# Zero matmuls ahead of the first scores, and new figures in the planner that orders the kernel

## The chip, the cores and the metric

The kernel runs on one core of a Trainium2 chip. The metric is the device time of one execution in microseconds, taken over several runs; 0.2% of it is about 1.7 us. A profile of one execution, taken separately, gives the rows below. PE is TensorE, DVE is VectorE, ACT is ScalarE, POOL is GpSimd and SP is SyncE, which here issues the DMAs.

## The reference

Three steps follow one another, all in float32:

```python
# q, k, v: 4 x 8 heads x 576 x 64; a window of 64 positions
scores = q @ k.T / 8, with -1e9 outside 0 <= i - j < 64
attn = softmax(scores)                        # max taken off, sum + 1e-9
x = (attn @ v), heads side by side            # 2304 x 512
h = x @ w_in;  x = (h * clip(h + 3, 0, 6) / 6) @ w_out     # 512 -> 2048 -> 512
h = x @ w2_in; out = max(0.01 * h, h) @ w2_out             # 512 -> 2048 -> 512
```

The weights arrive as float64 and are rounded on the chip.

## The kernel before, in words

Every float32 product is made of three matmuls on two halves of each operand (`...h` and `...l`). The attention is cut into 20 items (`items`), each one or two groups of 64 query positions of one batch. For an item, `scores` multiplies keys by queries into one or two PSUM banks. For the first nine items (`EARLY`) a mask matmul (L494, `ident_r` times `mask_r`) writes the mask into the bank first, and the scores (L507) add to it. `softmax` then takes the maximum (DVE L466, L467), the exponential (ACT L455), the sum (DVE L476), its reciprocal (DVE L462, L463), and normalises on POOL (L343). `st_P` transposes (L532) and `st_V` multiplies by the values (L564). 

The first layer follows block by block of tokens. Six chunks of 128 of the 2048 inner columns are done plainly (`st_h` L617, `st_y` L663), with the attention of later blocks between them. Their weights are loaded (`st`), rounded by DVE and ACT (`rounded`, L370 to L389) and parted into halves (`halves`, L332 and L342). The remaining chunks and the whole second layer are done in pairs by a scheme with seven instead of eight products (`paired`, L943, L1037, L1086, L1211); halves made once are kept in DRAM and loaded again.

Nothing of this is issued in the order in which it is written. Each step is put into a list (`Order.op`) with the engines that can do it and a cost for each, what it reads and writes, a delay after its end, and `later`, a list of steps that must have started before it. `Order.forward` then plays the list: again and again it takes the engine that can start something first, and on it the ready step with the earliest due time. `Order.backward` makes new due times from the outcome, and six such rounds are made. The best one is emitted, sorted by planned start, and that is the program order of every engine, each of which takes its instructions strictly in turn. The semaphores come from elsewhere: a framework follows the emitted instructions and makes each wait for earlier accesses to the same bytes of a tile. The plan itself knows only the reads and writes that a step names.

The planner's figures: an instruction of n columns costs 0.19 + 0.00083 n on ACT, 0.15 + 0.00104 n on DVE (half the slope for copies and scalar operations), 0.2 + 0.0024 n on POOL. A step starts 0.15 us after a step on another engine that it depends on, and 0.12 after one on its own engine for DVE and POOL. A load is 0.62 us on SP, then its bytes at 0.36 MB per us on one DMA engine, then a delay of 2.0.

Tiles come from rings. A ring can have homes: places inside other tiles that are free early on. The key tiles (`kt`) have two buffers of their own and two homes, in the token tile `xb` that later holds the first layer's output:

```python
late = sum(SIZES[:NB - 2])      # 1536
"kt": heads([(("home",), None, lambda i=i: xb(i, late, NK3)) for i in range(2)])   # NK3 = 768
```

`xb(c, o, n)` (with `XT` = 768) is columns c * 768 + (o mod 768) and on of tile number o // 768; there are `NPAIR` = 3 such tiles. The first identity and mask are made in tile 0 (L1326 to L1338). At the start SP issues loads of keys and queries for items 0 and 1, for item 2, of keys for items 3 and 4 (into the homes), then values and the first weights. Queries have two buffers.

Of the kernel before, what the change touches and what calls it, by code (L numbers as in the profile page):

```python
# [17 lines left out]
class Order:  # L18
# [5 lines left out]

    BIAS = 10.0
    LAG = 0.15

    class Buf:
        def __init__(self, pool, shape, dtype, tag, bufs):
# [32 lines left out]
    def op(self, ways, reads=(), writes=(), delay=0.0, chain=False, later=()):  # L62


        i = len(self.ops)
        deps, behind = set(), set(later)

        def whole(x):
            return x[0] if isinstance(x, tuple) and isinstance(x[0], self.Buf) else x

        def touch(b):
            if not b.ops:
                if b.prev is not None and b.prev[0] is not None:
                    behind.add(b.prev[0].ops[0])
                if b.prev is not None and b.prev[1] is not None:
                    deps.update(b.prev[1].ops)
            elif b.ops[0] != i:
                behind.add(b.ops[0])
            if not b.ops or b.ops[-1] != i:
                b.ops.append(i)  # L80

        for x in (*reads, *writes):
            b = whole(x)
            if isinstance(b, self.Buf):
                touch(b)
                if b.parent is not None:
                    touch(b.parent)
                if b.home is not None:
                    self.hist.setdefault(b.home, ([], []))[1].append(i)
        for x in reads:  # L90
            w, r = self.hist.setdefault(x, ([], []))
            deps.update(w)
            r.append(i)
        for x in writes:
            w, r = self.hist.setdefault(x, ([], []))
            deps.update(w + r)
            w.append(i)
        if chain:
            if self.last is not None:
                behind.add(self.last)  # L100
            self.last = i
        deps.discard(i)
        behind.discard(i)
        self.ops.append((ways, sorted(deps), sorted(behind - deps), delay))

    def lag(self, a, b):
        return (0.12 if a in ("DVE", "POOL") else 0.0) if a == b else self.LAG

    def forward(self, due):


        ops, after = self.ops, self.after
        n = len(ops)
        left = [len(deps) + len(behind) for _, deps, behind, _ in ops]
        ready, free, done, start, used = {}, {}, [0.0] * n, [0.0] * n, [0] * n

        def push(i):
            ways, deps, behind, _ = ops[i]
            for k, w in enumerate(ways):
                t = 0.0  # L120
                for d in deps:
                    t = max(t, done[d] + self.lag(ops[d][0][used[d]][0], w[0]))
                for d in behind:
                    t = max(t, start[d])
                ready.setdefault(w[0], {})[i] = (t, k)

        for i in range(n):
            if not left[i]:
                push(i)
        for _ in range(n):  # L130
            while True:
                e, t = min(
                    ((e, max(free.get(e, 0.0), min(x[0] for x in q.values()))) for e, q in ready.items() if q),
                    key=lambda x: x[1],
                )
                q = ready[e]
                i = min((j for j, x in q.items() if x[0] <= t), key=lambda j: (q[j][0] if e == "DMA" else due[j], j))
                r, k = ready[e][i]
                ways, _, _, delay = ops[i]
                best = min(  # L140
                    range(len(ways)), key=lambda m: max(free.get(ways[m][0], 0.0), r, t) + ways[m][1] + self.BIAS * m
                )
                if best == k:
                    break
                del ready[e][i]
            for w in ways:
                ready.get(w[0], {}).pop(i, None)
            start[i], used[i] = max(t, r), k
            free[e] = start[i] + ways[k][1]
            done[i] = free[e] + delay  # L150
            for s in after[i] + self.then[i]:
                left[s] -= 1
                if not left[s]:
                    push(s)
        return start, used, max(done)

    def backward(self, start, used, end):
# [8 lines left out]
        def push(i):  # L166
            t = end - ops[i][3]
            for s in after[i]:
                t = min(t, late[s] - self.lag(eng[i], eng[s]) - ops[i][3])
            for s in then[i]:  # L170
                t = min(t, late[s] + cost[i])
            ready.setdefault(eng[i], {})[i] = t
# [4 lines left out]
        for _ in range(n):  # L177
            e, t = max(
                ((e, min(free.get(e, end), max(q.values()))) for e, q in ready.items() if q), key=lambda x: x[1]
            )  # L180
            i = max((j for j, x in ready[e].items() if x >= t), key=lambda j: (start[j] + cost[j], j))
            del ready[e][i]
            late[i] = free[e] = t - cost[i]
            for d in ops[i][1] + ops[i][2]:
                left[d] -= 1
                if not left[d]:
                    push(d)
# [36 lines left out]
def swa_relu6_leaky_kernel(ctx: ExitStack, tc: tile.TileContext, q, k, v, w_in, w_out, w2_in, w2_out, out):  # L224
# [14 lines left out]
    nc = tc.nc  # L239
# [79 lines left out]
    def act(n, fn):  # L319
        return ("ACT", 0.19 + n * 0.00083, fn)  # L320

    def dve(n, fn, fast=False):
        return ("DVE", 0.15 + n * (0.00052 if fast else 0.00104), fn)

    def pool(n, fn):
        return ("POOL", 0.2 + n * 0.0024, fn)

    def pe(t, fn):
        return ("PE", t, fn)
# [9 lines left out]
        )  # L339

    def tensor_tensor(n, dst, a, b, alu, last=True):
        d = dve(n, lambda: nc.vector.tensor_tensor(out=dst(), in0=a(), in1=b(), op=alu))  # L342
        p = pool(n, lambda: nc.gpsimd.tensor_tensor(out=dst(), in0=a(), in1=b(), op=alu))  # L343
        return (d, p) if last else (p, d)

# [2 lines left out]

    def load(bytes_, dst, src, writes, reads=(), later=()):
        op([("SP", 0.62, lambda: nc.sync.dma_start(out=dst(), in_=src))], reads, writes, later=later)  # L350
        op([("DMA", bytes_ / 3.6e5, lambda: None)], (), writes, delay=2.0)

    def store(bytes_, dst, src, reads, writes):
        op([("SP", 0.62, lambda: nc.sync.dma_start(out=dst, in_=src()))], reads, writes)
        op([("DMA", bytes_ / 3.6e5, lambda: None)], reads, writes, delay=2.0)


    EXP_LO = float.fromhex("0x1.2p-15")
# [3 lines left out]
    def rounded(src, later=()):  # L362
# [14 lines left out]
        def af():  # L377
# [7 lines left out]
        op([ts(a, a, 3, 0x3FFFFFFF, ALU.logical_shift_left, ALU.bitwise_and)], [a], [a])  # L385
        op([dve(DM, lambda: nc.vector.scalar_tensor_tensor(  # L386
            out=a(), in0=high(), scalar=0xC0000000, in1=a(), op0=ALU.bitwise_and, op1=ALU.bitwise_or
        ))], [a, st], [a])
        op([act(DM, lambda: nc.scalar.activation(  # L389
            out=r(), in_=st()[:, :, 0], func=AF.Copy, scale=2.0 ** -29  # L390
        ))], [st], [r])
# [41 lines left out]
    def softmax(L, pp, early, apart):  # L433
# [24 lines left out]
                    **({} if apart else {"accum_out": sm()[:, c:c + 1]}),  # L458
                )

        def recips():
            nc.vector.tensor_scalar(out=rc(), in0=sm(), scalar1=1e-9, scalar2=None, op0=ALU.add)  # L462
            nc.vector.reciprocal(out=rc(), in_=rc())  # L463

        def greatest():
            nc.vector.tensor_reduce(out=nb(), in_=p3(), axis=AX.X, op=ALU.max)  # L466
            nc.vector.tensor_scalar(out=nb(), in0=nb(), scalar1=-SCALE, scalar2=None, op0=ALU.mult)  # L467

        if early:
            op([("DVE", 0.31 + NP * L * 0.00104, greatest)], [pp], [nb])  # L470
        else:
            op([("DVE", NP * (0.23 + L * 0.00104), low)], [pp], [s, nb])
        src = [pp, nb] if early else [s, nb]
        if apart:
            op([("ACT", NP * (0.2 + L * 0.00083), exps)], src, [s])
            op([dve(NP * L, lambda: nc.vector.tensor_reduce(out=sm(), in_=sv(), axis=AX.X, op=ALU.add))], [s], [sm])  # L476
        else:
            op([("ACT", NP * (0.3 + L * 0.00083), exps)], src, [s, sm])
        op([("DVE", 0.35, recips)], [sm], [rc])
        op(tensor_tensor(NP * L, sv, sv, lambda: rc().unsqueeze(2).to_broadcast([P, NP, L]), ALU.mult, False),  # L480
           [s, rc], [s])
        return s, sv
# [1 line left out]
    def scores(n, pps):  # L484
# [8 lines left out]
        for pp in pps if early else ():  # L493
# [1 line left out]
                pp()[:, 0:NP * L].rearrange("p (c l) -> p c l", c=NP), ident_r,  # L495
                mask_r[:, P - L:P].unsqueeze(1).to_broadcast([P, NP, L]), start=True, stop=True,
                skip_group_check=True,
            ))], writes=[pp])

        def fn():  # L500
            for c in range(NP):
# [10 lines left out]

        return 0.25 + NP * 0.222 * L / P, fn, [x, y], pps

    def st_S(n, pps):
        cost, fn, reads, writes = scores(n, pps)
        op([pe(cost, fn)], reads, writes)
        softmaxes(n, pps)

    def softmaxes(n, pps):  # L520
# [82 lines left out]
    def st_h(idx):  # L603
# [28 lines left out]
        def gg():  # L632
# [11 lines left out]
        op(copy(n, gg, rr, True, 1.0 / 6.0), [r], [gh])  # L644
        op([dve(n, lambda: nc.vector.scalar_tensor_tensor(
            out=gl()[:, 0:n], in0=rr(), scalar=1.0 / 6.0, in1=gg().bitcast(F32), op0=ALU.mult, op1=ALU.subtract
        ))], [r, gh], [gl])
        gs[idx] = (gh, gl)

    def st_y(idx):  # L650
# [161 lines left out]
    def paired():  # L812
# [340 lines left out]
        def outputs2(p, n, pairs):  # L1153
# [104 lines left out]
                todo.append(go)  # L1258
            return todo

        kk = 0
        turn_ = 0
        todo, plan = [], FILL[0]
# [56 lines left out]


    zero = const.tile([P, 1], F32, name="zero")
    nc.vector.memset(zero, 0.0)
    nc.scalar.activation(out=zero, in_=zero, func=AF.Exp)
    ident_f, mask_f = xb(0, 0, P), xb(0, P, P)
# [28 lines left out]
    for b in range(1, NB):  # L1354
        of[b] = [n for n in of[b] if n not in of[b - 1]]
    ahead = of[0]
    st_S(0, y_banks(0))
    st_S(1, y_banks(1))
    for n in ahead:
        st_P(n, banks("h", n))  # L1360
        st_V(n, bank("a", 2))
# [87 lines left out]
```

## Time and profile before

| | us |
|---|---|
| median of 3 runs (lowest, highest) | 834.54 (834.23, 834.97) |
| the profiled execution | 833.62 |
| its span, from the first to the last instruction | 831.8 |
| PE busy | 815.5 |
| DVE busy | 663.1 |
| ACT busy | 537.9 |
| POOL busy | 41.0 |

The span is the part of the time that the trace sees. An engine's busy time counts its compute instructions; PE's matmuls are pipelined and their ends are modelled. Times in the rows are from the span's start.

### The profile page before, as it was taken

To read this page: it belongs to the slowest core of one execution; us is meant where nothing else is said; L and a number is where in the kernel's file an instruction comes from. 1 tells how busy PE (TensorE), PEld (TensorE's weight loads), DVE (VectorE), ACT (ScalarE), POOL (GpSimd) and SP (SyncE) were. 2 spreads that over 40 slices of the span, in tenths; PEclk is the share of its full clock that TensorE was granted. 3 is DMA by queue.
4 is the path that set the end of the run, shared out by engine and by line. 5 is a ranking of instruction groups with operands and counts; after the bars stand their busy time and mean duration, and the time that the engine had idled before them with its cause. 6 is when DMAs were issued, how large, how long until landed. Compare 5 with 4: busy or idle time off the path is not lost.

```text
span 831.8 us, 16109 instructions
## 1 busy us (share of the span) xinstructions
PE 815.5 (98%) x5686; PEld 747.2 (90%) x5686; DVE 663.1 (80%) x1442; ACT 537.9 (65%) x1218; POOL 41.0 (5%) x45
## 2 busy tenths in 40 slices
PE   6799999999999999999999999999999999999998
PEld 5577888888999999999999988998999999999998
DVE  6999887788757888878888867898866688866766
ACT  5988888776666666657567646877674456555541
POOL 3222221210000000000000000000000000000000
PEclk9999999999999999999999999999999999999999
DMA  7976494648685879998899875788898787987735
GB/s 240 350 271 204 130 341 152 216 153 279 226 329 191 297 265 374 326 377 300 291 378 350 301 272 203 279 285 297 283 361 265 243 255 242 308 269 238 247 127 177
DMA packets 133792, 222.32 MB, mean 267 GB/s; under 512 B 12112, under 2 KB 55632, under 8 KB 133712
## 3 DMA queue, kind: packets, MB, share of 16 engines
q1 hardware_dynamic: 133712, 221.30, 77.9%
q8 instruction: 45, 0.74, 0.4%
q14 instruction: 35, 0.29, 0.1%
HBM read 165.94 MB, written 55.31 MB: 266 GB/s over the span
## 4 chain that ended last, share of the span: by engine, by line
PE 93%; DMA 3%; DVE 2%; ACT 1%; issue 0%; SPq 0%; POOL 0%; POOLq 0%; ACTq 0%; DVEq 0%
PE h L943 28%; PE y L1211 14%; PE y L1037 10%; PE y L663 9%; PE h L617 8%; PE a L943 6%; PE y L1086 5%; PE a L1037 5%; PE a L1086 3%; PE h L564 1%; PE a L532 1%; DMA qt<-in_q_dram 1%; PE a L507 1%; DMA xd<-xa 1%; DMA xb<-in_v_dram 0%; PE y L507 0%
## 5 line engine op out<-in xcount | busy, mean ns | idle before, releaser
L943 PE MATMUL h<-e,w0l 128*128 128x384 f32 x306 | 90.4, 335 | 0.0
L943 PE MATMUL h<-e,w0h 128*128 128x384 f32 x270 | 82.0, 335 | 0.0
L1037 PE MATMUL y<-at,w1h 128*128 128x512 f32 x240 | 79.4, 391 | 0.0
L370 DVE TENSOR_SCALAR ca<-ca 128x512 uint32<-128x512 uint32 (+1 forms) x128 | 55.9, 449 | 7.8 <-ACT ca L381 6.7
L332 ACT ACTIVATE qt<-h 128x384 f32<-128x384 f32 x65 | 31.7, 488 | 45.3 <-PE h L943 44.7
L943 PE MATMUL h<-xa,w0l 128*128 128x384 f32 x204 | 59.3, 335 | 0.0
L347 DVE TENSOR_TENSOR qt<-h,qt 128x384 f32<-128x384 f32 x57 | 31.7, 556 | 32.5 <-PE h L943 18.7
L943 PEld LDWEIGHTS h<-e,w0l 128*128 128x128 f32 x306 | 56.5, 188 | 0.4
L943 PE MATMUL h<-xa,w0h 128*128 128x384 f32 x180 | 54.1, 335 | 0.0
L1037 PEld LDWEIGHTS y<-at,w1h 128*128 128x128 f32 x240 | 45.1, 188 | 8.8
L943 PEld LDWEIGHTS h<-e,w0h 128*128 128x128 f32 x270 | 50.0, 188 | 0.4
L381 ACT ACTIVATE ca<-st 128x512 f32<-128x512 f32 x64 | 42.3, 665 | 11.0 <-DMA st<-in_moe_w_out_dram 4.1
L1037 PE MATMUL a<-at,w1h 128*128 128x256 f32 x240 | 47.8, 282 | 0.0
L1037 PE MATMUL y<-at,w1l 128*128 128x512 f32 x120 | 47.2, 394 | 0.0
L389 ACT ACTIVATE cr<-st 128x512 uint32<-128x512 uint32 x64 | 42.4, 670 | 7.2 <-DMA st<-in_moe_w_out_dram 3.8
L343 POOL TENSOR_TENSOR at<-at,rc 128x512 f32<-128x512 f32 (+1 forms) x36 | 39.7, 1103 | 137.5 <-DVE rc L463 89.7
L663 PE MATMUL y<-gh,w1h 128*128 128x512 f32 (+1 forms) x120 | 45.6, 380 | 0.0
L342 DVE CUSTOM_DVE_ANT_0 ca<-ca,cr 128x1024 uint16<-128x1024 uint16 x64 | 44.8, 707 | 0.9 <-ACT cr L389 0.6
L386 DVE SCALAR_TENSOR_TENSOR ca<-st,ca 128x512 uint32<-128x512 uint32 x64 | 44.5, 701 | 0.6
L663 PE MATMUL y<-gl,w1h 128*128 128x512 f32 (+1 forms) x120 | 44.4, 370 | 0.1
L663 PE MATMUL y<-gh,w1l 128*128 128x512 f32 (+1 forms) x120 | 44.3, 369 | 0.0
L332 ACT ACTIVATE at<-qt 128x384 fp32r<-128x384 f32 x69 | 35.9, 521 | 9.3 <-DVE qt L906 6.3
(379 smaller groups left out, 2421.0 us busy)
## 6 DMA issues: line engine op xcount, KB each, us to landing
w0h<-kept SPq DMA_DIRECT2D x116, 256.0 KB, 4.4
w0l<-kept SPq DMA_DIRECT2D x115, 256.0 KB, 4.4
w1h<-kept SPq DMA_DIRECT2D x76, 256.0 KB, 4.2
w1l<-kept SPq DMA_DIRECT2D x76, 256.0 KB, 4.4
st<-in_moe_w_in_dram SPq DMA_DIRECT2D x32, 512.0 KB, 6.2
st<-in_moe_w_out_dram SPq DMA_DIRECT2D x32, 512.0 KB, 5.1
kept<-e SPq DMA_DIRECT2D x33, 256.0 KB, 3.9
kept<-gh SPq DMA_DIRECT2D x30, 256.0 KB, 4.9
```

What stands on the lines that cost most here:

```text
L332: a = act(n, lambda: nc.scalar.activation(out=dst(), in_=src(), func=AF.Copy, scale=scale))
L342: d = dve(n, lambda: nc.vector.tensor_tensor(out=dst(), in0=a(), in1=b(), op=alu))
L370: return dve(DM, lambda: nc.vector.tensor_scalar(out=dst(), in0=src(), scalar1=s1, scalar2=s2, op0=op0, **({"op1": op1} if op1 else {})), ...
L381: act(DM, lambda: nc.scalar.activation(out=af(), in_=high().bitcast(F32), func=AF.Abs)),
L386: op([dve(DM, lambda: nc.vector.scalar_tensor_tensor(out=a(), in0=high(), scalar=0xC0000000, in1=a(), op0=ALU.bitwise_and, op1=ALU.bitwise ...
L389: op([act(DM, lambda: nc.scalar.activation(out=r(), in_=st()[:, :, 0], func=AF.Copy, scale=2.0 ** -29))], [st], [r])
L617: nc.tensor.matmul(ph()[:, 0:n], wt()[:, cs], xt()[:, 0:n], start=(c == 0 and m == 0), stop=(c == NK - 1 and m == 2),)
L663: nc.tensor.matmul(y()[:, 0:n], stat()[:, cs], mov()[:, 0:n], start=(first and m == 0), stop=(last and m == 2))
L943: nc.tensor.matmul(bk()[:, 0:HT], a, b_(), start=(start and j == 0 and q_ == 0), stop=(j == 1 and q_ == 2), skip_group_check=True,)
L1037: nc.tensor.matmul(y()[:, d:d + n], a()[:, cs], b_[1]()[:, t0:t0 + n], start=(begins and m == 0), stop=(last and m1 and m == 2), skip_grou ...
L1086: nc.tensor.matmul(y(), a()[:, cs], b_(), start=(first and m == 0), stop=(last and m == 2))
L1211: nc.tensor.matmul(y()[:, 256 * k:256 * k + 256], a()[:, cs], b_, start=(start and k == 0 and e == 0 and q_ == 0), stop=(e == 1 and q_ == ...
```

## The change

A block of 128 columns, `blank`, is taken from the last `xb` tile and set to zero by DVE before anything else. Twelve matmuls of 128 x 128 by 128 on it write into a spare PSUM bank that nothing reads: three before the first mask matmul, four that may start when the third mask matmul has started, five that may start when the first scores have started.

```diff
+    blank = xbt[NPAIR - 1]()[:, 0:P]
+    nc.vector.memset(blank, 0.0)
     nc.vector.memset(zero, 0.0)
...
+    spare = bank("h", 2)
+
+    def warm(n, cost, later=()):
+        def fn():
+            for _ in range(n):
+                nc.tensor.matmul(spare()[:, 0:P], blank, blank, start=True, stop=True, skip_group_check=True)
+
+        op([pe(cost, fn)], [], [spare], later=later)
+        return len(od.ops) - 1
+
+    heat.append(warm(3, 2.5))
     st_S(0, y_banks(0))
     st_S(1, y_banks(1))
+    for _ in range(4):
+        warm(1, 0.43, cold[:3])
+    for _ in range(5):
+        warm(1, 0.22, [first_scores])
```

`heat` holds the first of these steps, `cold` the mask matmuls, which now name `heat` as `later`; `first_scores` is the step of item 0's scores.

The planner gets new figures. A step marked as using the shared port (a fourth entry) waits until the other engine of DVE and POOL is 0.14 us from the end of its own marked step: all of POOL's, and on DVE the fast ones and those with two tensors to read. DVE's and ACT's next step may start 0.08 and 0.12 us before the end of the last. The third load in an unbroken row costs 1.3 more, the first 1.5 more. POOL costs 0.19 + 0.00168 n. All but the port and the rates hold only for steps before `late`, which is set where `paired` begins to list its own steps; behind it the lag of 0.12 and a DMA delay of 1.2 + 0.8 hold.

```diff
+    TAIL = {"DVE": 0.08, "ACT": 0.12}
+    STALL = 1.3
...
-    def lag(self, a, b):
-        return (0.12 if a in ("DVE", "POOL") else 0.0) if a == b else self.LAG
+    def lag(self, a, b, late=False):
+        return ((0.12 if late else 0.03) if a in ("DVE", "POOL") else 0.0) if a == b else self.LAG
...
+        def at(i, x):
+            w = ops[i][0][x[1]]
+            return max(x[0], port["POOL" if w[0] == "DVE" else "DVE"]) if len(w) > 3 else x[0]
...
-            free[e] = start[i] + ways[k][1]
-            done[i] = free[e] + delay
+            more = 0.0
+            if e == "DMA":
+                behind = behind + 1 if start[i] < free.get(e, 0.0) + 0.3 else 0
+                more = self.STALL if behind == 2 and i < self.late else 1.5 if e not in free else 0.0
+            done[i] = start[i] + ways[k][1] + more + delay
+            free[e] = start[i] + ways[k][1] + more - (self.TAIL.get(e, 0.0) if i < self.late else 0.0)
+            if len(ways[k]) > 3:
+                port[e] = done[i] - 0.14
...
-        op([("DMA", bytes_ / 3.6e5, lambda: None)], (), writes, delay=2.0)
+        op([("DMA", bytes_ / 3.55e5, lambda: None)], (), writes, delay=1.2)
...
+        od.late, od.more = len(od.ops), {"DMA": 0.8}
```

In `softmax` the maximum and its scaling, and the sum's offset and its reciprocal, which were one step each, become two steps each, with the same instructions.

## Rows read from the trace of the kernel before

**Rows 1.** The page's engine table: busy us, share of the span, instructions.
```profile
PE 815.5 (98%) x5686; PEld 747.2 (90%) x5686; DVE 663.1 (80%) x1442; ACT 537.9 (65%) x1218; POOL 41.0 (5%) x45
```

**Rows 2.** Busy time by window: window, us, each engine's busy us, clock, DMA.
```profile
8.62:10.78 2.16, 1.54 (x33) 1.05 (x34) 2.06 (x7) 1.20 (x5) 0.00 (x0) 1.00 0.95 271
10.78:16.87 6.09, 4.38 (x61) 2.99 (x61) 5.88 (x18) 4.69 (x16) 3.12 (x4) 1.00 0.94 327
16.87:30.00 13.13, 9.60 (x172) 7.79 (x172) 11.79 (x30) 11.92 (x31) 6.10 (x6) 1.00 0.77 261
30.00:68.00 38.00, 35.22 (x357) 25.83 (x354) 36.79 (x77) 33.23 (x101) 7.80 (x7) 1.00 0.85 300
68.00:230.00 162.00, 162.00 (x1352) 135.50 (x1353) 130.77 (x386) 128.32 (x348) 22.64 (x20) 1.00 0.63 212
230.00:600.00 370.00, 370.00 (x2041) 343.03 (x2040) 308.25 (x600) 238.88 (x475) 0.00 (x0) 1.00 0.85 300
600.00:832.00 232.00, 228.07 (x1628) 227.46 (x1626) 166.17 (x324) 117.26 (x241) 0.00 (x0) 1.00 0.77 249
```

**Rows 3.** PE's waits before 80 us: total us, times, longest.
```profile
PE h L532 <- POOL at L343: 2.7, 4, 1.1
PE y L507 <- DMA qt<-in_q_dram: 2.6, 3, 1.3
PE y L494 <- DVE mask_r L1338: 2.6, 1, 2.6
PE h L617 <- DVE w0l L342: 1.3, 2, 1.0
```

**Rows 4.** The chain of waits to 30 us: start, us, what.
```profile
1.49 4.12 DMA qt<-in_q_dram
...
10.50 6.32 DMA qt<-in_q_dram
```

**Rows 5.** The timeline to 10 us: start, us, instruction, idle time before it.
```profile
1.44 0.29 DVE L1327 CAST ident_r<-xb 128x128 fp32r<-128x128 f32 x1 [0.57 <-POOL xb masks.py:199]
...
2.55 1.86 PE L494 MATMUL y<-mask_r,ident_r 128*128 128x256 f32 x4 [2.55 <-DVE mask_r L1338]
...
3.42 1.22 SPq L350 DMA_DIRECT2D xb<-in_k_dram x2
...
5.75 2.82 PE L507 MATMUL y<-kt,qt 64*64 64x64 f32 x48 [1.33 <-DMA qt<-in_q_dram]
...
7.63 0.93 ACT L455 ACTIVATE at<-y,nb 128x64 f32<-128x64 f32 x4 [5.40 <-DVE nb L467]
...
8.62 0.50 PE L494 MATMUL y<-mask_r,ident_r 128*128 128x512 f32 x1
...
9.05 1.10 PE L507 MATMUL y<-kt,qt 64*64 64x128 f32 x32
```

**Rows 6.** DMA issued from 3.3 to 3.9: tile, engine, KB, us to landing.
```profile
xb<-in_k_dram SPq DMA_DIRECT2D x1, 384.0 KB, 7.1
```

**Rows 7.** Windows at the span's end, columns as in rows 2.
```profile
828.00:829.00 1.00, 0.07 (x1) 0.00 (x0) 0.51 (x2) 0.00 (x0) 0.00 (x0) 1.00 0.98 337
...
831.00:832.00 1.00, 0.00 (x0) 0.00 (x0) 0.00 (x0) 0.00 (x0) 0.00 (x0) 0.53 0.00 0
```

**Rows 8.** DVE's groups, four of 8.6:68, then two of 230:600: busy us, mean ns.
```profile
L370 DVE TENSOR_SCALAR ca<-ca 128x512 f32<-128x512 f32 x9 | 5.9, 666 | 0.0
L342 DVE TENSOR_TENSOR w0l<-ca,w0h 128x512 fp32r<-128x512 f32 x5 | 4.2, 849 | 0.0
L342 DVE TENSOR_TENSOR w1l<-ca,w1h 128x512 fp32r<-128x512 f32 x4 | 4.2, 1054 | 0.7 <-ACT w1h L332 0.7
L370 DVE TENSOR_SCALAR ca<-ca 128x512 uint32<-128x512 uint32 x9 | 4.7, 545 | 0.1
...
L370 DVE TENSOR_SCALAR ca<-ca 128x512 f32<-128x512 f32 x38 | 15.7, 422 | 5.0 <-ACT ca L381 4.7
L342 DVE TENSOR_TENSOR w1l<-ca,w1h 128x512 fp32r<-128x512 f32 x12 | 8.2, 686 | 0.7 <-ACT w1h L332 0.7
```

More of the change, by code (lines that the diff above doesn't have):

```diff
@@ L26 @@
     LAG = 0.15
+    TAIL = {"DVE": 0.08, "ACT": 0.12}
+    STALL = 1.3
+    more = {}
+    late = 1 << 30
     class Buf:
@@ L103, in op @@
         behind.discard(i)
-        self.ops.append((ways, sorted(deps), sorted(behind - deps), delay))
-    def lag(self, a, b):
-        return (0.12 if a in ("DVE", "POOL") else 0.0) if a == b else self.LAG
+        self.ops.append((ways, sorted(deps), sorted(behind - deps), delay + self.more.get(ways[0][0], 0.0)))
+    def lag(self, a, b, late=False):
+        return ((0.12 if late else 0.03) if a in ("DVE", "POOL") else 0.0) if a == b else self.LAG
     def forward(self, due):
@@ L115, in forward @@
         ready, free, done, start, used = {}, {}, [0.0] * n, [0.0] * n, [0] * n
+        port = {"DVE": 0.0, "POOL": 0.0}
+        behind = 0
+        def at(i, x):
+            w = ops[i][0][x[1]]
+            return max(x[0], port["POOL" if w[0] == "DVE" else "DVE"]) if len(w) > 3 else x[0]
         def push(i):
@@ L121, in push @@
                 for d in deps:
-                    t = max(t, done[d] + self.lag(ops[d][0][used[d]][0], w[0]))
+                    t = max(t, done[d] + self.lag(ops[d][0][used[d]][0], w[0], i >= self.late))
                 for d in behind:
@@ L132, in forward @@
                 e, t = min(
-                    ((e, max(free.get(e, 0.0), min(x[0] for x in q.values()))) for e, q in ready.items() if q),
-                    key=lambda x: x[1],
+                    ((e, max(free.get(e, 0.0), min(at(j, x) for j, x in q.items()))) for e, q in ready.items() if q),
+                    key=lambda x: (x[1], x[0] != "POOL"),
                 )
                 q = ready[e]
-                i = min((j for j, x in q.items() if x[0] <= t), key=lambda j: (q[j][0] if e == "DMA" else due[j], j))
-                r, k = ready[e][i]
+                i = min((j for j, x in q.items() if at(j, x) <= t), key=lambda j: (q[j][0] if e == "DMA" else due[j], j))
+                k = ready[e][i][1]
+                r = at(i, ready[e][i])
                 ways, _, _, delay = ops[i]
@@ L168, in push @@
             for s in after[i]:
-                t = min(t, late[s] - self.lag(eng[i], eng[s]) - ops[i][3])
+                t = min(t, late[s] - self.lag(eng[i], eng[s], i >= self.late) - ops[i][3])
             for s in then[i]:
@@ L182, in backward @@
             del ready[e][i]
-            late[i] = free[e] = t - cost[i]
+            late[i] = t - cost[i]
+            free[e] = late[i] + (self.TAIL.get(e, 0.0) if i < self.late else 0.0)
             for d in ops[i][1] + ops[i][2]:
@@ L320, in act, with dve @@
         return ("ACT", 0.19 + n * 0.00083, fn)
-    def dve(n, fn, fast=False):
-        return ("DVE", 0.15 + n * (0.00052 if fast else 0.00104), fn)
+    def dve(n, fn, fast=False, port=False):
+        way = ("DVE", 0.15 + n * (0.00052 if fast else 0.00104), fn)
+        return (*way, True) if fast or port else way
     def pool(n, fn):
-        return ("POOL", 0.2 + n * 0.0024, fn)
+        return ("POOL", 0.19 + n * 0.00168, fn, True)
     def pe(t, fn):
@@ L341, in tensor_tensor @@
     def tensor_tensor(n, dst, a, b, alu, last=True):
-        d = dve(n, lambda: nc.vector.tensor_tensor(out=dst(), in0=a(), in1=b(), op=alu))
+        d = dve(n, lambda: nc.vector.tensor_tensor(out=dst(), in0=a(), in1=b(), op=alu), port=True)
         p = pool(n, lambda: nc.gpsimd.tensor_tensor(out=dst(), in0=a(), in1=b(), op=alu))
@@ L350, in load @@
         op([("SP", 0.62, lambda: nc.sync.dma_start(out=dst(), in_=src))], reads, writes, later=later)
-        op([("DMA", bytes_ / 3.6e5, lambda: None)], (), writes, delay=2.0)
+        op([("DMA", bytes_ / 3.55e5, lambda: None)], (), writes, delay=1.2)
     def store(bytes_, dst, src, reads, writes):
         op([("SP", 0.62, lambda: nc.sync.dma_start(out=dst, in_=src()))], reads, writes)
-        op([("DMA", bytes_ / 3.6e5, lambda: None)], reads, writes, delay=2.0)
+        op([("DMA", bytes_ / 3.55e5, lambda: None)], reads, writes, delay=1.2)
     EXP_LO = float.fromhex("0x1.2p-15")
@@ L387, in rounded @@
             out=a(), in0=high(), scalar=0xC0000000, in1=a(), op0=ALU.bitwise_and, op1=ALU.bitwise_or
-        ))], [a, st], [a])
+        ), port=True)], [a, st], [a])
         op([act(DM, lambda: nc.scalar.activation(
@@ L459, in exps, with small @@
                 )
-        def recips():
-            nc.vector.tensor_scalar(out=rc(), in0=sm(), scalar1=1e-9, scalar2=None, op0=ALU.add)
-            nc.vector.reciprocal(out=rc(), in_=rc())
+        def small(t, s, k, alu):
+            op([("DVE", 0.17, lambda: nc.vector.tensor_scalar(
+                out=t(), in0=s(), scalar1=k, scalar2=None, op0=alu), True)], [s], [t])
         def greatest():
             nc.vector.tensor_reduce(out=nb(), in_=p3(), axis=AX.X, op=ALU.max)
-            nc.vector.tensor_scalar(out=nb(), in0=nb(), scalar1=-SCALE, scalar2=None, op0=ALU.mult)
         if early:
-            op([("DVE", 0.31 + NP * L * 0.00104, greatest)], [pp], [nb])
+            op([("DVE", 0.15 + NP * L * 0.00104, greatest)], [pp], [nb])
+            small(nb, nb, -SCALE, ALU.mult)
         else:
@@ L474, in softmax @@
         if apart:
-            op([("ACT", NP * (0.2 + L * 0.00083), exps)], src, [s])
+            op([("ACT", NP * (0.18 + L * 0.00083), exps)], src, [s])
             op([dve(NP * L, lambda: nc.vector.tensor_reduce(out=sm(), in_=sv(), axis=AX.X, op=ALU.add))], [s], [sm])
         else:
-            op([("ACT", NP * (0.3 + L * 0.00083), exps)], src, [s, sm])
-        op([("DVE", 0.35, recips)], [sm], [rc])
+            op([("ACT", NP * (0.27 + L * 0.00083), exps)], src, [s, sm])
+        small(rc, sm, 1e-9, ALU.add)
+        op([("DVE", 0.18, lambda: nc.vector.reciprocal(out=rc(), in_=rc()))], [rc], [rc])
         op(tensor_tensor(NP * L, sv, sv, lambda: rc().unsqueeze(2).to_broadcast([P, NP, L]), ALU.mult, False),
@@ L497, in scores @@
                 skip_group_check=True,
-            ))], writes=[pp])
+            ))], writes=[pp], later=heat)
+            cold.append(len(od.ops) - 1)
         def fn():
@@ L513, in scores @@
         return 0.25 + NP * 0.222 * L / P, fn, [x, y], pps
+    heat, cold, first_scores = [], [], 0
     def st_S(n, pps):
+        nonlocal first_scores
         cost, fn, reads, writes = scores(n, pps)
         op([pe(cost, fn)], reads, writes)
+        first_scores = first_scores or len(od.ops) - 1
         softmaxes(n, pps)
@@ L646, in st_h @@
             out=gl()[:, 0:n], in0=rr(), scalar=1.0 / 6.0, in1=gg().bitcast(F32), op0=ALU.mult, op1=ALU.subtract
-        ))], [r, gh], [gl])
+        ), port=True)], [r, gh], [gl])
         gs[idx] = (gh, gl)
```

## The prediction

> **What bounds the kernel now.** I read the page's table of engines first: PE is busy 98% of the span, so only what is left idle, or moves earlier, can be won [rows 1]. Where it is idle is seen in the windows [rows 2]: from 68 to 600 us PE is busy in every microsecond of the rows, and the last stretch lacks 232.00 - 228.07 = 3.9 us at the very end. The rest lies before 68: from 8.62 to 68 the rows lack 0.62 + 1.71 + 3.53 + 2.78 = 8.64 us, and PE's first useful scores start only at 5.75. In the same four stretches DVE lacks only 0.10 + 0.21 + 1.34 + 1.21 = 2.86 us, so there DVE sets the pace and PE waits for what hangs on it. The table of PE's waits then says for whom: mask and queries at the very start, POOL's normalisation 2.7 us, the queries' load again, and one late weight half of 1.0 us [rows 3]. The chain of waits has two long DMA pieces near the start, the first queries (landed at 5.61) and the queries issued at 10.50 that land at 16.82 [rows 4]. So the change has at most some 10 us to win, all of it before 68, and whatever it loses there goes through to the end, because behind it PE has no slack to give it back.
>
> **The change, part by part.** The sum is made against the profiled execution, 833.62 us (span 831.8 and 1.8 around it); the median of the runs is 834.54, and the same difference is put on that.
>
> *The memset and the first three zero matmuls.* DVE's memset of 128 columns lies in the 0.57 us for which DVE sits idle before its cast at 1.44, until POOL's first select is done [rows 5]; it costs nothing, and if that cover were gone, at most about those 0.57. The three matmuls stand in PE's queue before the mask matmuls, which start at 2.55. The mask matmuls (4 in 1.86, 0.47 each) are the nearest row from PE's start; the 32 score matmuls at 9.05 (1.10, 0.034 each) are the lower bound [rows 5]. From about 1.1 the three last until 1.2 to 2.5: nothing is late by them.
>
> *The next four zero matmuls: an unplanned wait.* This is the term that decides. The zeros are read from `blank`, columns 0 to 127 of the last `xb` tile. The same columns are the third home of the ring of key tiles (`xb(0, late, NK3)`, late = 1536 = 2 x 768, so that tile from column 0). The plan gives the new matmuls no read of `blank`, hence knows nothing of it. By the plan's times the SP issues are 0.62 apart and the load into that home is the fifth of six that nothing holds back, so it starts at 2.48 or earlier; the four zeros may start only behind the third mask matmul, at 3.0 or later (2.5 for the first zeros, 0.25 for each mask matmul). So in program order the load that overwrites the zeros comes first, and the four read what it wrote. That reads of one view of an `xb` tile wait for writes through another view is seen in this trace: DVE's cast of the identity waited for POOL's select on `xb` [rows 5]. The load is issued at 3.42 (second of a pair in one row) and lands 7.1 us later, at 10.5 [rows 5, 6]. PE takes its instructions in order, and behind the waiting zero stand the scores of items 0 and 1; behind these DVE's maxima, ACT's exponentials, and on SP the third load of queries, which needs the buffer that item 1's scores read, and behind that load every later load of values and weights in SP's queue.
>
> How much later the scores end: now they run from 5.75 for 2.82 us, to 8.57 [rows 5]. Their pace doubles just after: 32 matmuls of 128 columns take 1.10 at 9.05, while these 48 (32 of 128 columns, 16 of 64) take 2.82 where about 1.5 would do at the later pace. The clock column of the windows says 1.00 there too, but the pace is that of the lower of the two levels (1.2 against 2.4 GHz). After the change, starting at 10.5: at the low level 4 x 0.47 + 2.82 = 4.7, end 15.2, 6.65 late; at the full level 4 x 0.034 + 1.5 = 1.6, end 12.1, 3.6 late. I take the middle, 5.1, since PE will have run without a break from about 1.1 to 4.7 and then have rested until 10.5, and no row has such a pair. That a rest lowers the clock is seen at the end of the trace: PE is busy for only the first 0.07 us after 828, and in the last microsecond the mean granted clock is 0.53 [rows 7].
>
> The Trainium skill, "TensorE: Matmul & The Clock Gate", section "HAM oscillation — how this bites in real kernels", says that an engine left waiting for a DMA between two bursts is put back to half rate and begins the next burst slow. By it the shift is the upper end and the total 838.5; the end of this trace agrees, at 0.53.
>
> *The last five zeros* may start behind the first scores and fill PE behind those of item 1, ahead of a mask matmul that needs ACT's first exponentials (0.93 from 7.63, so done at 8.56, while the mask starts at 8.62 [rows 5]). They take 5 x 0.034 = 0.17 to 5 x 0.47 = 2.35, and ACT's wait covers a part where PE is quick: between 0 and 2.35, I take 0.3, the end of the quick row.
>
> *What the wait gives back.* When the third load of queries goes out, the first seven loads have all landed, and the later queries need not queue: now they take 6.32 us from 10.50, and PE waited 1.0 for them at 16.87 [rows 3, 4]. That wait goes: -1.0 (between 0 and -1.3, all such waits after 8.62).
>
> *The plan's new figures up to the plain chunks* (a port that DVE and POOL share, shorter lags, tails by which the next instruction starts earlier, a stall of the third load in a row, POOL cheaper) and the split of two small DVE pairs into single steps change no instruction, only the order. What the port costs now: from 8.6 to 68 DVE's shifts and clips take 666 and 545 ns against 422 later, where POOL does nothing, and the two low halves 1054 and 849 against 686 [rows 8]. That is 9 x 0.244 + 9 x 0.123 + 4 x 0.368 + 5 x 0.163 = 2.2 + 1.1 + 1.5 + 0.8 = 5.6 us of DVE time in the stretch that DVE bounds: the most that a better order wins. The other end is a loss: one more gap like the largest there, 1.0 [rows 3]. I take a gain of 2.0, little over a third, because the plan's times for loads and scores part from the chip's by 5 us at the start.
>
> *The figures behind* (`late`, 0.8 us added to each DMA's delay) restore lags and delays of before: 1.2 + 0.8 = 2.0. What may change there is the order of loads and of DVE and ACT work; PE's order is chained and has no gap from 68 to 600 [rows 2]. Zero, hidden by PE's own work; a gain is excluded, as there is no gap to win, and the other end is the fourth rival's price.
>
> Sum: 5.1 + 0.3 - 1.0 - 2.0 = +2.4. Profiled 836.0, median 834.54 + 2.4 = **836.9**.
>
> **Rivals.**
> *First: the four zeros don't wait.* For it: nothing in the trace shows how a matmul on these columns is ordered; against it, the cast that waited for the select [rows 5]. Then they lie in PE's rest from 4.4 on and end at about 6, some 0.3 after the queries have landed; the scores run at the quick pace, 1.5 for 2.82: -1.0. With the order's -2.0: -3.0, **831.5**: faster. It decides from the point where no wait stands between the load at 3.42 and the fourth zero.
> *Second: the clock falls back in the rest* and stays low through both items' scores: shift 6.65 for 5.1, +1.55, **838.5**. For it [rows 7]; against it, the clock could rise again while the zeros run.
> *Third: the order gives it all back.* If 4.7 of the 5.6 us of port delays go: 5.1 + 0.3 - 1.0 - 4.7 = -0.3, **834.2**, no change. For it: DVE is the bound there and its delays are real; against it: DVE's whole stream starts 5 us later, with 2.86 us of rest to draw on.
> *Fourth: the dense part opens.* Lags of 0.03 for 0.12 let the plan place results just in time; with five gaps of the 1.0 us wait for a weight half [rows 3] it is 5.0 more, **841.9**. Against it: that stretch has none now [rows 2].
>
> **How the numbers follow.** 0.2% (1.7 us, about what a measurement of this kernel tells from no change) puts the bounds at 832.9 and 836.2. The forecast has 0.38; its own range, by the ends of the order's gain, is 834 to 840, and as it lies near the bound I count 0.27 of it slower and 0.11 the same. First rival 0.20: 0.16 faster, 0.04 the same. Second 0.16, slower. Third 0.20: 0.04 faster, 0.15 the same, 0.01 slower. Fourth 0.06, slower. Together faster 0.20, the same 0.30, slower 0.50. The range reaches down over most of the first rival and up past the second: 830.8 to 841.0 leaves out the far ends of the first and nearly all of the fourth, under 0.2.
>
> **What would show it.** In the changed kernel's chain of waits, PE's fourth zero matmul ends a wait of some 5 us for the load of keys into `xb`; PE is idle from about 4.7 to 10.5, the scores of item 0 start at 11 or later, and SP's third load of queries goes out at 12 to 15 for 8.65. If instead the scores start near 5.75 to 6.1 and take about 1.5, the first rival holds and I was wrong on the side. The second shows in the pace of the scores: 2.8 us for the 48. The order's share shows in the shifts of DVE near 422 ns before 68 and in PE's idle time from the scores to 68, now 8.64. Gaps on PE after 68 would show the fourth.

## The result, and the profile after

| | before | after |
|---|---|---|
| median, us (6 runs each, same chip) | 834.75 (834.23 to 838.45) | 841.77 (840.81 to 843.41) |
| the profiled execution | 833.62 | 840.81 |
| its span | 831.8 | 839.0 |
| PE busy | 815.5 | 819.0 |
| DVE busy | 663.1 | 656.2 |

The ratio is 1.0074 (95% interval 1.0058 to 1.0089): slower by 6.2 us by the ratio, 7.0 between the medians, clear of the 0.2%. The side and the mechanism were forecast, the size (+2.4) was not: 841.77 lies 0.8 above the range that was given (830.8 to 841.0), and 834.54 times the ratio, 840.7, lies 0.3 inside it.

PE's timeline of the changed kernel, as in [rows 5]; the line numbers are about 20 higher. The zeros are L1390, the scores L528, the mask L514; each zero is two instructions in the trace.

```profile
1.06 1.65 PE L1390 MATMUL h<-xb 128*128 128x128 f32 x6 [1.06 <-DVE zero L1351]
2.55 1.43 PE L514 MATMUL y<-mask_r,ident_r 128*128 128x256 f32 x3
10.32 1.65 PE L1390 MATMUL h<-xb 128*128 128x128 f32 x6 [6.34 <-DMA xb<-in_k_dram]
11.62 0.77 PE L514 MATMUL y<-mask_r,ident_r 128*128 128x512 f32 x1
12.19 0.63 PE L1390 MATMUL h<-xb 128*128 128x128 f32 x2
12.75 1.89 PE L528 MATMUL y<-kt,qt 64*64 64x64 f32 x48
14.57 1.16 PE L1390 MATMUL h<-xb 128*128 128x128 f32 x8
...
16.18 1.10 PE L528 MATMUL y<-kt,qt 64*64 64x128 f32 x32
```

The fourth zero (the first of the four) stands for 6.34 us until the keys have landed in its home, and behind it item 0's scores begin at 12.75 for 5.75, item 2's at 16.18 for 9.05: 7.13 us late. On SP the third load of queries waits for the scores and goes out at 14.74 for 8.65, and the values and weights behind it go with it:

```profile
3.48 1.23 SPq L369 DMA_DIRECT2D xb<-in_k_dram x2
...
14.74 0.34 SPq L369 DMA_DIRECT2D qt<-in_q_dram  x1
15.12 0.43 SPq L369 DMA_DIRECT2D at<-in_v_dram  x1
15.60 0.91 SPq L369 DMA_DIRECT2D xb<-in_v_dram  x2
17.37 0.33 SPq L369 DMA_DIRECT2D qt<-in_q_dram  x1
17.74 1.19 SPq L369 DMA_DIRECT2D st<-in_moe_w_in_dram  x1
```

What follows the scores is found in windows. From item 2's scores to 80 us and in the stretch behind the plain chunks, the changed kernel, then from item 2's scores the one before (window, length, busy us of PE, PEld, DVE, ACT, POOL):

```profile
16.18:80.00 63.82, 56.68 (x696) 43.74 (x695) 57.14 (x153) 58.96 (x176) 19.41 (x18) 1.00 0.84 287
240.00:600.00 360.00, 358.69 (x1973) 331.53 (x1973) 302.12 (x587) 233.06 (x461) 0.00 (x0) 1.00 0.84 297
```

```profile
9.05:80.00 70.95, 62.31 (x713) 47.08 (x713) 66.81 (x170) 62.69 (x183) 18.60 (x18) 1.00 0.80 276
```

PE idles 63.82 - 56.68 = 7.14 us for 70.95 - 62.31 = 8.64: the new order and the lighter DMA queue together give back 1.5. PE's waits for queries behind the first scores, 1.3 us before, are gone; a wait for values has come up that the kernel before has not:

```profile
PE a L589 <- DMA xb<-in_v_dram: 1.5, 1, 1.5
```

Against the gain, the stretch without a gap in [rows 2] now lacks 360.00 - 358.69 = 1.31. These are PE's waits from 80 us to the end (total, times, longest):

```profile
PE h L968 <- ACT w0h L351: 1.0, 1, 1.0
PE a L557 <- DVE nb L467: 0.4, 1, 0.4
PE h L968 <- DVE w0l L361: 0.3, 1, 0.3
```

So the span's +7.2 is +7.13 at item 2's scores, -1.5 from there to 80, and +1.7 behind it (7.3 by this count).

The port's share did change as the plan meant it. DVE's groups from 16 to 75 us, for [rows 8]:

```profile
L389 DVE TENSOR_SCALAR ca<-ca 128x512 uint32<-128x512 uint32 x11 | 4.4, 418 | 0.0
L389 DVE TENSOR_SCALAR ca<-ca 128x512 f32<-128x512 f32 x11 | 4.3, 418 | 0.4 <-ACT ca L400 0.3
L361 DVE TENSOR_TENSOR w1l<-ca,w1h 128x512 fp32r<-128x512 f32 x4 | 4.1, 1022 | 0.1
L361 DVE TENSOR_TENSOR w0l<-ca,w0h 128x512 fp32r<-128x512 f32 x5 | 4.1, 817 | 0.0
```

The shifts and clips run at 418 ns for 666 and 545; the low halves stay slow at 1022 and 817. One other group of nine (`CUSTOM_DVE_ANT_0`, L361) went the other way, 750 ns for 679.

### The profile page after: what moved, and what is told of

The parts are those of the page before. It is cut to its first block, busy times and chain, and to the rows that moved or that the text cites. A ratio compares the mean times of both kernels' runs of the same rounds, so it can differ in the third digit from the quotient of the medians.

```text
span 839.0 us, 16129 instructions
## 1 busy us (share of the span) xinstructions
PE 819.0 (98%) x5710; PEld 750.6 (89%) x5710; DVE 656.2 (78%) x1443; ACT 536.4 (64%) x1218; POOL 40.9 (5%) x45
## 4 chain that ended last, share of the span: by engine, by line
PE 94%; DMA 2%; DVE 2%; ACT 1%; issue 0%; SPq 0%; DVEq 0%; ACTq 0%
PE h L968 27%; PE y L1236 14%; PE y L1062 10%; PE y L688 9%; PE h L642 9%; PE a L968 6%; PE a L1062 5%; PE y L1111 5%; PE a L1111 2%; PE h L589 2%; PE a L528 1%; PE a L557 1%; DMA st<-in_moe_w_in_dram 1%; DMA xb<-in_k_dram 1%; ACT at L474 0%; DMA st<-in_moe_w_out_dram 0%
## 5 line engine op out<-in xcount | busy, mean ns | idle before, releaser
L389 DVE TENSOR_SCALAR ca<-ca 128x512 uint32<-128x512 uint32 (+1 forms) x128 | 52.1, 420 | 3.6 <-ACT ca L400 2.6
L361 DVE CUSTOM_DVE_ANT_0 ca<-ca,cr 128x1024 uint16<-128x1024 uint16 x64 | 45.7, 721 | 0.8
```

The costliest lines, as they stand in the source:

```text
L389: return dve(DM, lambda: nc.vector.tensor_scalar(out=dst(), in0=src(), scalar1=s1, scalar2=s2, op0=op0, **({"op1": op1} if op1 else {})), ...
```

## The experiments

Ratios are to the kernel before on the same chip in the same rounds, with their 95% intervals. In those rounds the kernel before itself had medians of 835.6 to 836.0; what goes with that is told under the hardware below. Theory W is that the zeros' wait for the load of keys is the loss; rival S is that the new figures order the work worse.

**The zeros moved** (the order of every engine's program is the same).

```diff
-    blank = xbt[NPAIR - 1]()[:, 0:P]
+    blank = xbt[1]()[:, 0:P]
```

> The changed kernel with its zeros in columns 0 to 127 of the second xb tile, where no load is put early; the program order of every engine is the same. Theory W (the zeros' wait for the load of keys is the whole loss): item 2's scores, now 16.18, start near 9.1 again, 7.1 us earlier, and the time falls by about 7, to 834.0 to 835.5. Rival S (the new figures order the work worse): the wait goes, but the time stays above 839, with the loss then in PE's idle time from the scores to 80 us or at 575 us.

Measured 835.43 us, ratio 0.9988 (0.9976 to 0.9999). From 1.0074 that is 0.0086 or 7.2 us for one address. PE's timeline:

```profile
3.77 1.48 PE L1390 MATMUL h<-xb 128*128 128x128 f32 x6
4.91 0.77 PE L514 MATMUL y<-mask_r,ident_r 128*128 128x512 f32 x1
5.48 0.47 PE L1390 MATMUL h<-xb 128*128 128x128 f32 x2
5.88 1.56 PE L528 MATMUL y<-kt,qt 64*64 64x64 f32 x48
...
9.55 1.10 PE L528 MATMUL y<-kt,qt 64*64 64x128 f32 x32 [0.52 <-DMA qt<-in_q_dram]
```

No wait, and the zeros do what their function's name (`warm`) says: the 48 scores take 1.56 us for 2.82. But item 2's scores are no earlier (9.55 for 9.05), because their queries land only then. The 1.3 us end in a wait for a DMA, and W holds against S. As the order is the same, the loss of the change is this wait and what follows from it.

**The new figures without zeros.** The memset, the twelve matmuls and their uses as `later` are taken out.

```diff
-    heat.append(warm(3, 2.5))
...
-    for _ in range(4):
-        warm(1, 0.43, cold[:3])
-    for _ in range(5):
-        warm(1, 0.22, [first_scores])
```

> The new figures alone: no zeros, no memset, no order of the mask matmuls behind them. W: as the kernel before within 1.7 us (833 to 836.5), with the scores of items 0 and 1 at the low pace, 2.8 us. S: 838 to 842, as slow as the changed kernel or nearly so.

836.07 us, ratio 1.0005 (0.9992 to 1.0018): no change, as W says. The figures are worth nothing here that can be measured, in either direction. Nor are the moved zeros beside them: 0.9988 with the zeros and 1.0005 without, with intervals that overlap.

**The zeros without the new figures.** The twelve matmuls on `xbt[1]` and their `later` lists in the kernel before; its planner is left as it was.

> The kernel before with its old figures, and the twelve zero matmuls read from the second xb tile, where no load overwrites them. If the zeros do what they are named for, the scores of items 0 and 1 run at the quick pace, 1.5 us for 2.8, and the time is 833.0 to 834.5; if the third load of queries sets the pace behind them, and not the scores, nothing of that is seen at the end: 834.75 within 1 us. W and S say the same of this one.

837.47 us, ratio 1.0020 (1.0006 to 1.0034): not faster, slightly slower, a miss for both numbers that were offered. The scores do end earlier, but item 2's start at 10.41, behind their queries, and with another list the plan is another one; its trace has PE waiting 3.3 us for queries from 10 us on, where it was 1.3 before, and 2.0 us for values at 30.86. How much of the loss are these waits and how much is the clock (below) stays open.

**The zeros on the other home**, whose load lands later.

```diff
-    blank = xbt[NPAIR - 1]()[:, 0:P]
+    blank = xbt[NPAIR - 1]()[:, XT:XT + P]
```

> The changed kernel with its zeros on the second home of the key ring (columns 768 to 895 of the last xb tile), whose load is issued one later and lands at about 11.8 for 10.5; the same program order. W: the wait of the fourth zero grows by 1.2 us and the time with it, to about 843.0 (842.3 to 843.7). S: no change from 841.8 beyond 0.5.

844.2 us, ratio 1.0098 (1.0077 to 1.0119), 0.0024 or 2.0 us over the changed kernel. The wait itself:

```profile
12.19 1.65 PE L1390 MATMUL h<-xb 128*128 128x128 f32 x6 [8.21 <-DMA xb<-in_k_dram]
```

It is 8.21 - 6.34 = 1.87 us longer and the span 2.8 longer; the load landed later than forecast, and time follows the wait. The other 0.9 goes with a wait of 1.0 us for ACT's `qt` at 497, which this execution has and the changed kernel's has not, in the same program order. The two ratios' intervals touch, so the size is rough; the rows are not.

**Without the four zeros ahead of the scores**, the five behind them still on the home.

```diff
-    for _ in range(4):
-        warm(1, 0.43, cold[:3])
```

> The changed kernel, zeros on the home of the key ring as there, without the four zeros ahead of the first scores; the three at the start and the five behind the scores stay. Theory W: the wait for the load of keys now stands behind the scores of items 0 and 1, which run from 5.75; it lasts from about 8 to 10.4, and item 2's scores start at about 12 for 16.2: some 2.5 us over the moved zeros, ratio 1.001 to 1.003. If the loss of the change were not that wait but the place of the zeros as such, it would stay at 1.007.

839.95 us, ratio 1.0059 (1.0037 to 1.0081): a good deal more than forecast. By the numbers that were offered this run speaks against W: its interval leaves out 1.001 to 1.003 and takes in 1.007, the figure for zeros that cost by their place as such. The trace does show the wait where it was forecast:

```profile
5.71 1.56 PE L528 MATMUL y<-kt,qt 64*64 64x64 f32 x48 [1.30 <-DMA qt<-in_q_dram]
10.06 1.16 PE L1390 MATMUL h<-xb 128*128 128x128 f32 x8 [2.79 <-DMA xb<-in_k_dram]
...
11.71 1.99 PE L528 MATMUL y<-kt,qt 64*64 64x128 f32 x32
```

The scores run quick, PE rests for 2.79 us, and then item 2's scores take 1.99 us where they took 1.10. The window from 11.40 has the granted clock at the lower level:

```profile
10.00:11.40 1.40, 1.34 (x10) 1.30 (x11) 0.00 (x0) 0.92 (x4) 0.16 (x1) 1.00 1.07 279
11.40:14.80 3.40, 3.40 (x39) 2.54 (x38) 1.07 (x2) 0.00 (x0) 0.00 (x0) 0.51 0.65 204
14.80:16.00 1.20, 0.76 (x10) 0.40 (x10) 1.20 (x5) 0.83 (x3) 0.00 (x0) 0.98 0.85 225
```

The section that the prediction cited from the Trainium skill ("TensorE: Matmul & The Clock Gate", section "HAM oscillation — how this bites in real kernels") says that a wait for a DMA puts the engine back to half rate and that the next burst starts slow. The trace agrees that the rate fell to half behind the wait, 1.99 against 1.10; it does not agree that the burst started slow, for its first 1.34 us, with four zeros in 1.16, had 1.00.

Item 2's scores end at 13.70, 3.0 later than with the zeros moved (10.65). The profiled executions differ by 2.3 (838.45 for 836.19), the ratios by 0.0071 or 5.9 us. What makes up the rest of the size is not shown.

**The wait alone**, in the kernel before with its old figures: one matmul more.

```diff
+            if n == 0:
+                blank = xbt[NPAIR - 1]()[:, 0:P]
+                nc.tensor.matmul(spare()[:, 0:P], blank, blank, start=True, stop=True, skip_group_check=True)
             for c in range(NP):
```

> The kernel before with one matmul more, ahead of item 0's scores, that reads columns 0 to 127 of the last xb tile: the wait for the load of keys alone, with the old figures and no other matmul added; the order of all else is that of before. Theory W: PE waits from 4.4 to about 10.4, the scores of items 0 and 1 end near 13.7 for 8.57 at the low pace, and the time rises by 5.1 less at most 1.0 for the queries' wait: ratio 1.0045 to 1.0065. If the wait were hidden by the loads behind it, below 1.002.

840.46 us, ratio 1.0060 (1.0036 to 1.0084), inside the forecast, without anything else of the change. PE's timeline:

```profile
2.54 1.86 PE L494 MATMUL y<-mask_r,ident_r 128*128 128x256 f32 x4 [2.54 <-DVE mask_r L1341]
8.76 0.80 PE L503 MATMUL h<-xb 128*128 128x128 f32 x2 [4.36 <-DMA xb<-in_k_dram]
9.49 2.83 PE L510 MATMUL y<-kt,qt 64*64 64x64 f32 x48
```

The load landed at 8.76 in this execution, earlier than in the others, hence a wait of 4.36 rather than 6. Item 2's scores start at 13.06 for 9.05, 4.0 late, yet the span is 6.0 longer (837.8 for 831.8). So the ratio is as forecast, but not by the forecast's sum. From item 2's scores to 80 us PE idles 6.78 for 8.64, 1.9 less. Behind that it waits twice where the kernel before, whose order of instructions this is, waits for nothing, and from 33 to 36 the granted clock was 0.57 for 1.00:

```profile
PE h L946 <- ACT qt L927: 1.4, 1, 1.4
PE h L946 <- ACT wx L332: 0.9, 1, 0.9
33.00:36.00 3.00, 3.00 (x49) 2.51 (x44) 1.40 (x3) 2.21 (x6) 0.00 (x0) 0.57 1.02 404
```

That is 4.0 - 1.9 + 2.3 = 4.4; the 1.6 left stand beside the lower clock, and that it makes all of them is not shown.

Five more asked how the moved zeros, or the kernel before, could be made better. None of the edits made either faster.

**The DMA rate put back behind the plain chunks**, with the zeros moved.

```diff
-        op([("DMA", bytes_ / 3.55e5, lambda: None)], (), writes, delay=1.2)
+        op([("DMA", bytes_ / od.rate, lambda: None)], (), writes, delay=1.2)
...
-        od.late, od.more = len(od.ops), {"DMA": 0.8}
+        od.late, od.more, od.rate = len(od.ops), {"DMA": 0.8}, 3.6e5
```

> The zeros on the second xb tile, and the one figure that the change did not put back behind the plain chunks, the DMA rate, put back there (0.36 for 0.355 MB per us). With the zeros moved, PE still waits 1.0 us at 490 and 1.3 us at 571 us for ACT, where the kernel before waits for nothing. Theory L (these late waits come from the figures behind): both go, 2.3 us less than with the zeros moved alone, ratio to before 0.995 to 0.997. Rival C (any change of the list makes another order, and such waits come and go with it): the waits differ but don't vanish together, ratio 0.998 to 1.001.

837.46 us, ratio 1.0023 (1.0010 to 1.0036). The wait at 490 went, the one at 571 stayed (1.03 and 0.56 at 572), and the early order changed with them. Theory L falls, and the ratio is above rival C's range too.

**0.3 us more delay for ACT's steps in the plan**, with the zeros moved: `od.more` is `{"DMA": 0.8, "ACT": 0.3}`.

> The zeros on the second xb tile, and behind the plain chunks 0.3 us added to the delay of every ACT step in the plan, beside the 0.8 for DMAs. Theory L (the late waits at 490 and 571 us come from ACT results planned too tightly): both go, ratio 0.995 to 0.9975, faster than the kernel before. Rival C (each new list gives another order, whose waits nobody planned): some wait of about 1 us remains in the stretch from 240 to 600, ratio 0.998 to 1.002.

837.52 us, ratio 1.0017 (1.0000 to 1.0033). The waits at 490 and 571 are gone and others stand at 319 (0.83) and 555 (0.50). This is as rival C has it: the waits change with the list. The list is not all: the changed kernel, the moved zeros and the other home run one program order, and their traces have late waits of 1.7, 2.3 and 2.7 us.

**Zeros to fill PE's rests**, with the zeros moved; the same in the kernel before; and with the last edit.

```diff
+    def fill(n, to, k):
+        for _ in range(k if n < 5 else 0):
+            nc.tensor.matmul(to()[:, 0:P], blank, blank, start=True, stop=True, skip_group_check=True)
...
             def fn(sv=sv, pp=pp):
+                fill(n, pp, 1)
...
         def fn():
+            fill(n, po, 2)
             for j, vv in enumerate(vs):
```

> The zeros on the second xb tile, and besides one zero matmul ahead of each transposition and two ahead of each product with values of the first five items, into the bank that they then overwrite; the plan does not know of them (19 more, some 4.6 us of PE at 0.24 each, in a stretch from 13 to 33 us where PE idles 6.5). Theory K (the rests of PE at 20 to 30 us are what lowers the granted clock for 6.8 us at 29.6): the clock stays at the full level from its rise to the end, PE's matmuls at 30 to 36 us run twice as fast, and the time is 1 to 2.5 us below that with the zeros moved alone, ratio 0.996 to 0.998. Rival: the added zeros stand in front of work that is ready, and cost what the clock gives, ratio 0.999 to 1.004.

> The kernel before with its old figures and no zeros at the start, and with the zeros of the fill alone (one ahead of each transposition, two ahead of each product with values, first five items). Theory K: runs in which the mean granted clock is below 0.999 (21 of 29 so far) don't come up any more, and the median falls by 1 to 2, ratio 0.997 to 0.999. Rival: the clock still falls, or the zeros cost as much as it gives, ratio 0.999 to 1.004.

> As the last one, with the fill of zeros ahead of transpositions and products with values of the first five items. If both theories hold, the clock stays up in more of the runs and the late waits are gone: ratio 0.994 to 0.997. If the fill gives back nothing, as with the moved zeros (1.0000 against 0.9988), the ratio is that of the last one or 0.001 over it.

Ratios 1.0000 (0.9986 to 1.0014), 1.0026 (1.0012 to 1.0041) and 1.0025 (1.0008 to 1.0041). Runs with a mean clock below 0.999 were 5 of 12, 5 of 12 and 3 of 12, against 6 of 12 with the zeros moved and 17 of 29 and 18 of 23 of the kernel before in the same rounds: fewer, but they did not stop, and the times did not fall. The last fill against the same kernel without it is the clearest pair, 3 of 12 for 10 of 12, with the median at 837.8 for 837.5. Theory K is not shown, and the fill is no remedy.

## Why the prediction was right, and where its sizes were not

- *The unplanned wait*: right, in place, in order and in what stood behind it. Shown with one program order: without the wait the time is that of before (0.9988), with a later load it is 1.0098. The wait alone, at 1.0060, agrees, but part of that time lies behind 30 us. One reading was off: the load into this home is the first of its pair, not the second.
- *The shift*: forecast 5.1 for the scores' end plus 0.3 for the five zeros, 5.4 in all; measured 7.13 at item 2's scores. The scores of items 0 and 1 ended 6.1 late (14.6 for 8.57), between the two ends: 4.3 us after the landing, for 1.6 to 4.7. PE had run only to 3.98, not 4.7, because a mask matmul stands behind the first of these zeros; behind the wait the first three zeros took 1.65, as much as the three at the start. From the scores' end to item 2's scores it is 1.5 for 0.5, the other 1.0, with the five zeros in between: the term of 0.3 was their quick end, while four zeros took 1.16, 0.29 each and not 0.034. That lower bound came from score matmuls of 64*64; a zero is 128*128 and shows as two instructions.
- *What the wait gives back* (1.0) and *the order's gain* (2.0): 1.5 together. The wait for queries did go, but the wait of 1.5 for values came. The port's part was right in its rows, 418 ns, but DVE's busy time is not PE's: with 3.4 us less in the shifts and clips, PE idled 1.5 less, the lighter DMA queue included. Without zeros (1.0005) the new figures gain nothing, so 2.0 was too much.
- *The figures behind*: zero was wrong. 1.7 us of waits came up behind 80 us, for ACT's and DVE's results. With either figure that was tried some of them go and others come. That they belong to the new order is not shown: the wait alone has 2.3 us of them in the order of before. What brings them stays open; the step that failed is that PE's own work hides what changes there.
- *First three zeros*: nothing late by them, right; they ran from 1.06 to 2.7.
- *Rivals*: the first (the zeros don't wait) is the moved kernel, priced at 831.5 or -3.0; it measures 0.9988 or -1.0. Its -1.0 for quick scores stops at item 2, whose scores wait for their queries until 9.55, and its -2.0 for the order did not come. The second (the clock stays low) did not happen in full: the scores took 1.89 and ended at 14.6, not 15.2. The third needed 4.7 of gain where 1.5 came. Of the fourth, waits of 1.7 in all for 5.0.

The forecast sum with the measured terms is 7.1 - 1.5 + 1.7 = 7.3, for 7.2 in the profiled span. All three sizes were off to the same side, by 1.7, 1.5 and 1.7.

## What to carry to other kernels

A planner that orders instructions by declared reads and writes must be told of every read, a dummy's too: here a buffer that nobody needs to be zero was the landing place of a load planned earlier, and the order of issue turned filler into the critical wait. Put the operands of such filler where nothing else writes, and before spending on a faster start, look at what the next step waits for: a score stage 1.3 us shorter brought nothing clear of the noise, as the queries behind it landed no earlier. Small waits of about 1 us come and go here with the edits of the list, and also between kernels that share one order, so an effect of that size needs the order held fixed and many runs.

## What the runs showed of the hardware

The granted clock fell again in the middle of the kernel, in many executions. With the zeros moved, the windows around 30 us show it (the last three columns: clock, DMA share, GB/s):

```profile
29.00:30.00 1.00, 1.00 (x26) 0.98 (x28) 0.90 (x3) 0.70 (x2) 0.00 (x0) 0.78 1.02 418
30.00:33.00 3.00, 2.27 (x30) 1.74 (x26) 1.45 (x4) 1.73 (x4) 0.00 (x0) 0.50 1.06 384
33.00:36.00 3.00, 3.00 (x7) 2.32 (x8) 3.00 (x7) 3.00 (x7) 0.00 (x0) 0.50 1.06 262
36.00:37.00 1.00, 1.00 (x5) 0.81 (x4) 1.00 (x3) 1.00 (x6) 0.00 (x0) 0.81 1.04 389
```

PE had waited 0.92, 0.61 and 1.39 us just before, at 24.55, 26.87 and 28.92. The kernel before showed nothing of it in the trace above, but of its 29 runs beside the first set 21 had a mean clock below 0.999; they took 836.5 us on average, the other 8 took 834.3. All six runs of the changed kernel had 0.999 or more. Much of the spread of the kernel before, 832.6 to 838.1, goes with it (the 8 lie from 832.6 to 835.3, the 21 from 835.0 to 838.1), so one edit can look 2 us better or worse in a single profile. Whether such rests set it off stays open: with the fill the fall came less often and did not end, and the time did not fall with it.

Landing times at the start also moved between executions with the same loads issued: the first home's keys landed 6.8 us after issue in the changed kernel, 7.1 in the one before, and 5.3 in the kernel with the wait alone.
